# Attention feeding a channel mixer on one core: a fixed order of pieces in place of a planner, shared PSUM buffers, 1/rms by row tiles, q of two more batches by DMA transpose

## The chip, the cores and the metric

The kernel runs on one core of one Trainium2 chip. The metric is the time of one execution on the device in microseconds (us). Each kernel was run several times; a table gives the median and the range. The profile is one execution of its own; its span is about 2 us shorter than the reported time. An execution counts as slow when it is over 1.5% above the fastest of the same kernel; comparisons use the fast ones, and slow ones are pointed out.

Names used below: PE is the matrix engine, DVE the vector engine, ACT the scalar engine, POOL the engine that issues most loads, SP the engine that issues stores and DMA transposes. A "filler" is an idle matmul on zeros, whose only purpose is to keep PE's clock at full speed.

## The reference

Eight batches of eight heads; 576 positions; head size 64; so x has 8 × 576 rows of 512. All inputs and the output are float32.

```python
def attn(q, k, v, g_norm):                       # q, k, v: (8, 8, 576, 64)
    kv  = einsum('bhsd,bhse->bhde', k, v)        # 64 x 64 per head
    out = einsum('bhsd,bhde->bhse', q, kv)       # called u below
    rms = sqrt(mean(out * out, -1) + 1e-6)
    return out / rms * g_norm

def mixer(x, mu_k, mu_r, w_k, w_v, w_r):         # x: (8, 576, 512), from attn
    x_prev = x shifted by one position, zeros first
    xk = mu_k * x + (1 - mu_k) * x_prev
    xr = mu_r * x + (1 - mu_r) * x_prev
    k  = relu(xk @ w_k)                          # w_k: 512 x 1024
    v  = (k * k) @ w_v                           # w_v: 1024 x 512
    r  = sigmoid(xr @ w_r)                       # w_r: 512 x 512
    return r * v
```

## The kernel before

Matmuls run in bf16. Attention works by batch (0 to 7), the mixer by group of 512 rows (0 to 8), each as soon as its rows of xk and xr are there. In the text, "K of group 2" is the matmul of w_k with group 2's xk, "R" the one with w_r, "V" the one with w_v, and "u of batch 2" the matmuls of q with kv.

Every operation is a "piece" with its engine, its cost in us, what it depends on and the buffers it uses. A planner runs through the pieces with a list-scheduling model and decides the order, the engine of pieces that can go on either of two, and the buffers.

```python
class Planner:
    LAT = {"PE": 0.25, "ACT": 0.15, "DVE": 0.12, "POOL": 0.15, "SP": 0.0}
    ...
    def run(self, warm=None):
        ...  # picks the ready piece with the earliest start, then the earliest due time
             # puts fillers where PE would idle (before the first R, and until 80 us)

BUFS = { ...
    "mm": (2, (128, 2, 512), FP32),     # PSUM of the mixer
    "at": (2, (128, 2, 512), FP32),     # PSUM of attention
}
```

q has to be transposed before u. Batches 0 to 3 do that on PE, with a copy out of PSUM; batches 4 to 7 with a DMA transpose issued by SP:

```python
DMA_T = 4
...
if b >= DMA_T:
    def q_dma(_):
        nc.sync.dma_start_transpose(out=get(qT)..., in_=qin.t...)
else:
    for hp in hps:
        ...  nc.tensor.transpose(...)    # PE, into PSUM
        ...  copy(eng, get(qT)[...], ps.t[...])
```

1/rms is built from column sums of u squared (a matmul with a selector), Ln and Exp on ACT, and a matmul with a 0/1 selector that spreads it over all rows; DVE then multiplies three operands:

```python
nc.scalar.activation(out=get(ln), in_=pst.t[:, 0, 0:SEC], func=AF.Ln, bias=eps, scale=1.0 / HD)
nc.scalar.activation(out=get(rs), in_=ln.t, func=AF.Exp, scale=-0.5)
...
nc.tensor.matmul(get(ps)[:, i, SEC*c:SEC*c+SEC], selg[:, tl, sub]..., rs.t, start=True, stop=True)  # 144 columns each
nc.vector.scalar_tensor_tensor(out=xT..., in0=uT..., scalar=g_col, in1=ps..., op0=ALU.mult, op1=ALU.mult)
```

The run starts with loads by POOL, which also change float32 to bf16, and with fillers on PE:

```python
def idle(n, buf):
    for _ in range(n):
        nc.tensor.matmul(get(buf or warm)[:, 0, :], zeros[:, 0:128], zeros, start=True, stop=True)

plan.run((5.0, p_first, 80.0, idle))
```

## Time and profile before

| | before |
|---|---|
| time, median of 3 runs | 224.23 us (224.2 to 224.51) |
| span of the profile | 222.2 us |
| first R starts | 25.75 us |
| last matmul ends | 217.95 us |
| PE idle between the two | 6.7 us |
| fillers | 52 matmuls, 15.3 us |

From the page of the kernel before: the busy time of each engine, then rows of 40 equal slices of the span. Each digit is a busy share in tenths; PEclk is PE's granted clock in tenths of full speed; DMA is the mean busy share of the 16 DMA engines.

```profile
span 222.2 us, 4055 instructions
PE 205.6 (93%) x1671; PEld 102.5 (46%) x1671; DVE 144.8 (65%) x253; ACT 124.1 (56%) x172; POOL 25.8 (12%) x39
...
PE   2989999798799989999999999999999999999971
...
PEclk9999999999999999999999999999999999999999
DMA  5999999999999999999950420051033033033033
```

PE is busy nearly all the time, and at full clock from 10.7 us on. Before that the trace has no record of the clock, and the page draws a 9 there; six fillers took 2.74 us at 4.78 us, 0.46 us each, where later ones take 0.22. DMA is full for the first half of the run, then has slack. So PE is the limit, with the first 25 us and the DMA-full half as the places where something else can hold it up.

From the timeline of PE in the kernel before (start, duration, line, operands, shapes and count; in brackets the idle time before it and what ended that):

```profile
20.79 5.13 PE L620 MATMUL mm<-zeros 128*128 128x512 bf16 x23
25.75 1.89 PE L571 MATMUL mm<-w_r,xr 128*128 128x512 bf16 x8
28.01 0.95 PE L361 MATMUL at<-v,k 96*64 96x64 bf16 x48 [0.36 <-DMA v<-in_v_dram]
...
41.77 0.95 PE L361 MATMUL at<-v,k 96*64 96x64 bf16 x48 [1.22 <-DMA v<-in_v_dram]
...
72.83 1.89 PE L548 MATMUL mm<-xk,w_k 128*128 128x512 bf16 x8
```

The first R stands behind 23 fillers. Its data came in parts: the last xr that these eight matmuls read was written at 25.55 us (timeline of DVE). Batches 1 and 2 wait for their loads. K of group 2 starts at 72.83 us.

The chain of work that ended last (start, duration, what) has two DMA steps in the first 80 us, a load of q and a DMA transpose:

```profile
16.50 28.14 DMA q<-in_q_dram
...
63.59 12.60 DMA qT<-q
```

### The profile page before, as it was taken

To read this page: it belongs to the slowest core of one execution; us is meant where nothing else is said; L and a number is where in the kernel's file an instruction comes from. 1 tells how busy PE (TensorE), PEld (TensorE's weight loads), DVE (VectorE), ACT (ScalarE), POOL (GpSimd) and SP (SyncE) were. 2 spreads that over 40 slices of the span, in tenths; PEclk is the share of its full clock that TensorE was granted. 3 is DMA by queue.
4 is the path that set the end of the run, shared out by engine and by line. 5 is a ranking of instruction groups with operands and counts; after the bars stand their busy time and mean duration, and the time that the engine had idled before them with its cause. 6 is when DMAs were issued, how large, how long until landed. Compare 5 with 4: busy or idle time off the path is not lost.

```text
span 222.2 us, 4055 instructions
## 1 busy us (share of the span) xinstructions
PE 205.6 (93%) x1671; PEld 102.5 (46%) x1671; DVE 144.8 (65%) x253; ACT 124.1 (56%) x172; POOL 25.8 (12%) x39
## 2 busy tenths in 40 slices
PE   2989999798799989999999999999999999999971
PEld 1445454455354444545454694445444444444430
DVE  1159857358989999899679869976963143143131
ACT  5367647725948929776678277847716306405500
POOL 7861031210300500400000000000000000000000
PEclk9999999999999999999999999999999999999999
DMA  5999999999999999999950420051033033033033
GB/s 74 190 201 208 203 207 203 203 205 244 204 203 157 229 173 191 197 211 191 188 158 3 106 86 0 0 152 39 0 98 90 3 96 96 0 86 105 0 94 94
DMA packets 36150, 28.84 MB, mean 130 GB/s; under 512 B 11036, under 2 KB 31012, under 8 KB 36132
## 3 DMA queue, kind: packets, MB, share of 16 engines
q0 software_dynamic: 21008, 16.78, 49.3%
q1 hardware_dynamic: 15124, 11.81, 23.9%
q8 instruction: 13, 0.21, 0.4%
q14 instruction: 5, 0.04, 0.0%
HBM read 33.56 MB, written 9.44 MB: 193 GB/s over the span
## 4 chain that ended last, share of the span: by engine, by line
PE 71%; DMA 18%; DVE 6%; POOL 1%; issue 1%; ACT 0%; DVEq 0%; POOLq 0%
PE mm L591 27%; PE mm L548 22%; DMA q<-in_q_dram 13%; PE mm L571 11%; DMA qT<-q 6%; PE at L463 3%; PE mm L620 2%; PE at L411 2%; PE at L361 1%; DVE xT L471 1%; DVE out L595 1%; PE at L391 1%; PE at L440 1%; POOL k L294 1%; DVE sq L420 1%
## 5 line engine op out<-in xcount | busy, mean ns | idle before, releaser
L591 PE MATMUL mm<-w_v,sqk 128*128 128x512 bf16 x288 | 65.7, 379 | 1.7 <-DVE out L595 1.7
L548 PE MATMUL mm<-xk,w_k 128*128 128x512 bf16 (+1 forms) x320 | 66.1, 358 | 1.0 <-DVE xk L507 1.0
L552 ACT ACTIVATE relu<-mm 128x1024 bf16<-128x1024 f32 x36 | 36.7, 1024 | 44.5 <-PE mm L548 42.8
L548 PEld LDWEIGHTS <-w_k 128*128 128x128 bf16 x320 | 30.3, 98 | 29.6 <-issue 1.7
L591 PEld LDWEIGHTS <-sqk 128*128 128x128 bf16 x288 | 27.2, 98 | 34.1 <-issue 3.6
L555 DVE TENSOR_TENSOR sqk<-relu 128x1024 bf16<-128x1024 bf16 x36 | 24.7, 689 | 24.1 <-ACT relu L552 24.1
L595 DVE TENSOR_TENSOR out<-mm,sig 128x1024 f32<-128x1024 f32 (+1 forms) x20 | 22.1, 1116 | 24.9 <-PE mm L591 24.9
L571 PE MATMUL mm<-w_r,xr 128*128 128x512 bf16 x144 | 34.1, 379 | 0.0
L471 DVE SCALAR_TENSOR_TENSOR xT<-uT,mu_sb,at 128x576 bf16<-128x576 bf16 (+1 forms) x31 | 23.6, 791 | 3.0 <-PE at L463 2.7
L576 ACT ACTIVATE sig<-mm 128x1024 bf16<-128x1024 f32 x18 | 18.4, 1023 | 10.5 <-PE mm L571 10.4
L504 ACT ACTIVATE t<-d,mu_sb 128x576 bf16<-128x576 bf16 x30 | 21.0, 770 | 3.0 <-DVE xr L507 1.9
L571 PEld LDWEIGHTS <-xr 128*128 128x128 bf16 x144 | 13.3, 98 | 14.2
L221 ACT CAST uT<-at 128x576 bf16<-128x576 f32 x19 | 11.7, 637 | 9.4 <-PE at L411 9.4
L620 PE MATMUL mm<-zeros 128*128 128x512 bf16 x52 | 15.3, 423 | 0.0
L420 DVE TENSOR_TENSOR sq<-uT 128x576 bf16<-128x576 bf16 x32 | 13.3, 454 | 0.8 <-ACT uT L221 0.7
L294 POOL DMA_DIRECT2D k<-in_k_dram x10 | 7.5, 750 | 42.7 <-PE at L361 40.1
L463 PEld LDWEIGHTS <-selg 128*128 128x128 bf16 x128 | 9.6, 98 | 6.2 <-issue 1.2
L463 PE MATMUL at<-rs,selg 128*128 128x144 bf16 x120 | 11.1, 226 | 0.7 <-DVE xT L471 0.7
L507 DVE TENSOR_TENSOR xk<-t,xT 128x2304 bf16<-128x2304 bf16 (+2 forms) x10 | 11.2, 1118 | 0.4
L489 DVE TENSOR_TENSOR d<-xT 128x2304 bf16<-128x2304 bf16 (+2 forms) x10 | 11.2, 1119 | 0.3
L507 DVE TENSOR_TENSOR xr<-t,xT 128x2304 bf16<-128x2304 bf16 (+2 forms) x10 | 11.0, 1112 | 0.0
L502 DVE TENSOR_SCALAR t<-d,mu_sb 128x576 bf16<-128x576 bf16 x34 | 10.4, 368 | 0.2
(51 smaller groups left out, 133.1 us busy)
## 6 DMA issues: line engine op xcount, KB each, us to landing
out_dram<-out SPq DMA_DIRECT2D x24, 192.0 KB, 2.5
k<-in_k_dram POOLq DMA_DIRECT2D x7, 576.0 KB, 14.6
v<-in_v_dram POOLq DMA_DIRECT2D x7, 576.0 KB, 16.8
q<-in_q_dram POOLq DMA_DIRECT2D x7, 576.0 KB, 16.4
out_dram<-out SPq DMA_DIRECT2D x24, 128.0 KB, 2.4
out_dram<-out SPq DMA_DIRECT2D x24, 64.0 KB, 2.0
w_k<-in_moe_w_k_dram POOLq DMA_DIRECT2D x1, 1024.0 KB, 12.9
w_v<-in_moe_w_v_dram POOLq DMA_DIRECT2D x1, 1024.0 KB, 23.5
```

The lines of the kernel that those rows point to most:

```text
L463: nc.tensor.matmul(get(ps)[:, i, SEC * c:SEC * c + SEC], selg[:, tl, sub].rearrange("p e d -> p (e d)"), rs.t, start=True, stop=True)
L471: nc.vector.scalar_tensor_tensor(out=xT.t[:, hs, xs], in0=get(uT)[:, hs].rearrange("q h i jj p -> q h (i jj p)")[:, :, cs], scalar=g_col, ...
L504: nc.scalar.mul(out=dst, in_=d.t[:, hp, :], mul=by)
L507: nc.vector.tensor_tensor(out=dst[:, hsl, c0:c0 + S], in0=t.t[:, 0:n, :], in1=xT.t[:, hsl, 0:S], op=ALU.add)
L548: nc.tensor.matmul(get(ps)[:, fc % 2, a0:a1], w_k_sb[:, cc, 128 * fc:128 * fc + 128], xk[:, cc, x0:x0 + a1 - a0], start=(cc == 0), stop=(c ...
L552: nc.scalar.activation(out=get(rt), in_=ps.t, func=AF.Relu)
L555: nc.vector.tensor_mul(out=get(sqk)[:, 2 * f2:2 * f2 + 2, :], in0=rt.t, in1=rt.t)
L571: nc.tensor.matmul(get(ps)[:, ci % 2, :], xr[:, cc, n0:n0 + 128], w_r_sb[:, cc, :], start=(cc == 0), stop=(cc == NHP - 1))
L576: nc.scalar.activation(out=get(sg), in_=ps.t, func=AF.Sigmoid)
L591: nc.tensor.matmul(get(ps)[:, ci % 2, :], sqk.t[:, fc, 128 * ci:128 * ci + 128], w_v_sb[:, fc, :], start=(fc == 0), stop=(fc == NFC - 1))
L595: nc.vector.tensor_mul(out=get(ot)[:, xs, :], in0=ps.t[:, xs, :], in1=sg.t[:, xs, :])
L620: nc.tensor.matmul(get(buf or warm)[:, 0, :], zeros[:, 0:128], zeros, start=True, stop=True)
```

## The change

The intent, part by part:

1. The planner goes. A fixed list names every piece in order, with its engine and its buffer. The list was made ahead of time; the kernel only walks through it.
2. The two pairs of PSUM buffers become four that any piece may take.
3. Start: the first k and v come as float32 by the hardware queues of SP and ACT and are cast; 1/rms of batch 0 is done per head pair; R of group 0 accumulates head pair by head pair, so that it can begin before all of batch 0 is done.
4. 1/rms: one ACT function instead of Ln and Exp; sums and spreading as four row tiles (matmuls of 32 rows, 288 columns) instead of 144-column pieces; the factor g_norm moves into the selector, and DVE's three-operand multiply becomes a plain one.
5. q of batches 2 and 3 by DMA transpose too.
6. Few fillers: 25 at the start and 4 and 5 later, 224 columns each.

The diff, cut to its core:

```diff
-class Planner: ...
+ORDER = """
+    early_k::0 zero early_v::1 cast_v:A:0 cast_k:D:0 idle:25:0 kv0.0::0 load_k0.2 load_v0.2 ...
+    ... load_q0.2::0 load_q0.0 sel_load mu_load load_v0.4 ...
+    ... load_k2.0::0 load_v2.0::0 ... load_q2.0::0 ... qTd2::0 idle:5:0 V0.0a::0 ...
+    ... relu1.3::1 K1.5::3 u2.3::1 u2.2::2 ...
+"""                                  # 696 pieces: name:engine:buffers   (cut)
+class Plan:
+    def run(self, order, idle): ...  # walks through ORDER, checks dependencies and buffers
-    DMA_T = 4
+    DMA_T = 2
-        "mm": (2, (128, 2, 512), FP32),
-        "at": (2, (128, 2, 512), FP32),
+        "ps": (4, (128, 2, 512), FP32),
+    def load_early(n):               # first two heads of k and v: float32, then a cast
+        (nc.sync if eng == "SP" else nc.scalar).dma_start(out=raw..., in_=rows(n, 0, 0, 2))
-            nc.scalar.activation(out=get(ln), ..., func=AF.Ln, ...)
-            nc.scalar.activation(out=get(rs), in_=ln.t, func=AF.Exp, scale=-0.5)
+            nc.scalar.activation(out=get(rs)..., in_=get(pst)[:, :, 0:HS],
+                                 func=AF.Abs_reciprocal_sqrt, bias=1e-6, scale=1.0 / HD)
+            nc.tensor.matmul(get(pp[hp // 2])[:, hp % 2, 0:HS], sel[32*hp:32*hp+32]...,
+                             get(rs)[32*hp:32*hp+32, HS*half:HS*half+HS], start=True, stop=True)
-                    nc.vector.scalar_tensor_tensor(..., scalar=g_col, ..., op0=ALU.mult, op1=ALU.mult)
+                    nc.vector.tensor_tensor(..., op=ALU.mult)
+            for cc in range(NHP - 1):    # R of group 0, head pair by head pair
+                ms.append(add(f"R{g}.{cc}", ..., deps=ms[-1:] + [need["r"][cc], p_wr], bufs=pss))
-    plan.run((5.0, p_first, 80.0, idle))
+    plan.run(ORDER, idle)
```

## The prediction

> **What bounds the kernel now.** TensorE (PE 205.6 of 222.2 us in the busy-time table; DVE 65%, ACT 56%), in three stages.
> 1. Start: the first R matmul runs at 25.75 us (timeline); before it PE mostly runs 52 idle matmuls (15.3 us). From 15 to 25 us DVE is busy 9.65 us of 10 (windows): batch 0's norm chain is DVE-limited.
> 2. 25.75 to 217.97 us. The mixer's 720 matmuls at 0.864 us per four (chain of waits) are 155.5 us. The chain's increments give attention on PE: kv 0.88, u 0.8, sums 0.36, spreading 1/rms 1.1 per batch, PE transposes of q about 2.0 for batches 1 to 3; about 28 us. PE idles 5.0 us from 25.7 to 90 and twice 0.84 us in the tail, waiting for the output multiply.
> 3. End: 4.2 us from last matmul to end of span. The reported time is 2 us above the span.
>
> The DMA row is full to about 115 us at some 205 GB/s. kv of batch 2 waits for its load until 41.8 us; q of batch 2 lands at 44.6.
>
> **What the change does.**
> - Start: first loads by two hardware queues, 1/rms of batch 0 per head pair, R of group 0 per head pair. Batch 0 and w_r are 2.3 MB, 12 us at 205 GB/s after 3.5 us. DVE's list up to the last xr costs about 12 us by durations in the trace. Estimate: R starts at 16.5 us: -9.
> - PE: spreading takes four matmuls of 288 columns instead of eight of 144 per half; q of batches 2 and 3 goes to DMA transposes. I count 155.5 us mixer and 18.7 us attention from the first R on: -10.
> - DVE: x becomes a plain multiply (now 791 ns), squares go by two pairs (now 454 ns each). ACT: Ln plus Exp (0.70 us) become one. 13 table switches against 12 loads: nothing saved. Neither engine limits.
> - Shared PSUM buffers remove small waits only.
>
> **What is given back.** Loads carry the same bytes, so PE now runs into DMA. w_v lands at 34 to 36 us, when K of group 0 is done at about 30. q of batch 2 lands at 44.5; a DMA transpose took 12.6 to 15.2 us to land (DMA view), so u of batch 2 can't run before about 58, while the fixed order reaches it near 50. Batch 3's transpose queues behind (8 us of issue each). I expect 9 to 12 us of PE waits between 25 and 70 and K of group 2 starting near 69. Then 121 us mixer, 11.3 us attention, 1 us tail wait, 4.2 us end: span 205 (1 us taken off for overlap).
>
> **Predicted: 206.5 us, 8 in 10 from 199 to 212.** Faster by over 2%: 0.96; within 2%: 0.03; slower: 0.01.
>
> **What would show it.** Timeline: first R at 15 to 19 us, first K of group 2 at 65 to 71. Waits: several us of PE on DMA qT and w_v. After 70 us no PE gaps. PE filler about 5 us. DMA row full to about 110 us.
>
> **What would make it wrong.** If loads or transposes land earlier than the trace's rate says, the waits vanish: 197 to 199. If the fixed order, planned with modelled costs (relu 0.918 us where the trace has 1.02), stalls PE on PSUM or the in-order ACT and DVE queues: 210 or more. Few fillers may leave PE slow: the Trainium skill ("TensorE: Matmul & The Clock Gate", Part 1) says that after an idle window of about 3.4 us the clock halves; the first fillers here take 0.44 us against 0.22 later, which agrees. A cold R, or a cold stretch after the transpose wait, costs up to 1.7 us each.

The 1.7 us of its last sentence is an estimate: half of the page's window of 3.4 us.

## The result, and the profile after

| | before | after |
|---|---|---|
| time, median of 4 runs | 224.24 us (224.2 to 224.51) | 220.82 us (220.17 to 221.16) |
| ratio of fast runs, 95% interval | | 0.984 (0.982 to 0.986) |
| span of the profile | 222.2 us | 218.9 us |
| first R starts | 25.75 us | 20.85 us |
| K of group 2 starts | 72.83 us | 75.46 us |
| last matmul ends | 217.95 us | 213.38 us |
| mean granted PE clock | 1.000 | 0.946 |

Ratios here and below are the mean time of one kernel's fast runs over that of the kernel before in the same rounds, so they are not quite the ratio of the medians quoted. The change is 1.6% faster, which is within 2%; the prediction had 206.5 us and gave "within 2%" a chance of 0.03. It was wrong.

The same lines of the page, after:

```profile
span 218.9 us, 3677 instructions
PE 195.2 (89%) x1454; PEld 93.6 (43%) x1476; DVE 138.1 (63%) x251; ACT 125.2 (57%) x162; POOL 28.6 (13%) x45
...
PE   7277989999299999999988999999999999999970
...
PEclk9955799999859999999999999999999999999997
DMA  7999999999999990699999952220650004000485
```

PE has 10 us less to do, as busy time goes, but the span is only 3.3 us shorter. Two places catch the eye: PEclk falls to 5 in slices 3 and 4 (from about 11 to 22 us) and to 8 and 5 in slices 11 and 12 (55 to 66 us), and PE's row has a 2 in the first of these two (55 to 60 us).

The timeline of PE after:

```profile
11.33 0.56 PE L251 MATMUL ps<-ident,mu_raw 9*128 9x9 f32 x2 [2.73 <-DMA mu_raw<-in_moe_mu_r_dram]
...
21.70 3.69 PE L566 MATMUL ps<-w_r,xr 128*128 128x512 bf16 x10 [0.22 <-issue]
...
49.64 6.22 PE L544 MATMUL ps<-xk,w_k 128*128 128x512 bf16 x28
59.99 0.94 PE L392 MATMUL ps<-qT,kv 64*64 64x288 bf16 x12 [4.14 <-DMA qT<-q]
...
63.07 1.89 PE L600 MATMUL ps<-w_v,sqk 128*128 128x512 bf16 x4
...
69.67 1.04 PE L600 MATMUL ps<-w_v,sqk 128*128 128x512 bf16 x4
```

Three things are read here. A constants' transpose waits 2.73 us for a load. Ten matmuls of R take 3.69 us, where at full clock eight took 1.89 us before. And u of batch 2 (line 392) waits 4.14 us for the DMA transpose of q; the group of four matmuls 3 us later takes 1.89 us, and an equal one at 69.67, after the clock has come back, 1.04.

The chain of work that ended last, after:

```profile
42.24 1.96 PE ps L600 x9
44.20 15.75 DMA qT<-q
```

In the kernel before, the chain ran through the load of q to 44.6 us and then through PE; now it runs through the transpose until 59.95 us. The transposes' issue, from the timeline of SP after:

```profile
44.20 8.12 SPq L361 DMA_TRANSPOSE qT<-q  x1
54.54 2.06 SPq L526 DMA_DIRECT2D out_dram<-out  x4
56.83 14.38 SPq L361 DMA_TRANSPOSE qT<-q  x2
```

Stretches of both kernels: length, then busy time (and count) of PE, PE's weight loads, DVE, ACT and POOL, then granted clock, DMA share and GB/s. The kernel after:

```profile
10.00:25.00 15.00, 11.50 (x76) 5.89 (x78) 10.81 (x31) 9.85 (x19) 7.54 (x11) 0.54 1.27 202
...
40.00:60.00 20.00, 15.43 (x122) 6.79 (x121) 12.50 (x21) 9.79 (x13) 0.77 (x1) 0.96 1.31 190
60.00:80.00 20.00, 19.73 (x152) 8.11 (x155) 15.15 (x25) 10.90 (x15) 3.06 (x4) 0.86 1.17 195
```

The kernel before:

```profile
10.00:25.00 15.00, 13.65 (x128) 6.91 (x127) 11.37 (x28) 9.55 (x20) 5.50 (x7) 1.00 1.23 204
...
40.00:60.00 20.00, 16.21 (x229) 9.32 (x218) 14.01 (x25) 12.51 (x22) 3.83 (x5) 1.00 1.30 215
60.00:80.00 20.00, 19.15 (x198) 9.51 (x198) 18.53 (x34) 14.88 (x22) 3.80 (x4) 1.00 1.31 197
```

The 60 to 80 stretch shows why busy time misleads: PE is busier after than before (19.73 against 19.15 us), but at 0.86 of the clock. From 10 to 25 us PE is busy 77% of the time, and nearly all of it at half clock.

A balance of the span, all from the two timelines. "PE work" is busy time between the first R and the last matmul, with the cost of half clock taken out and given a row of its own. That cost is an estimate: half of the time at half clock after the first R (20.85 to 24.44 and 60.0 to 65.4 us), 4.5 us. The prediction's column is worked out from its own numbers.

| us | before | after | difference | predicted difference |
|---|---|---|---|---|
| first R starts | 25.75 | 20.85 | −4.9 | −9.2 |
| PE work from there | 185.5 | 177.6 | −7.9 | −11.3 |
| PE idle from there | 6.7 | 10.4 | +3.7 | +3.9 |
| half clock from there (estimate) | 0 | 4.5 | +4.5 | 0 |
| last matmul to the end | 4.25 | 5.5 | +1.3 | 0 |
| span | 222.2 | 218.9 | −3.3 | −16.7 |

One caution about the row "PE work". In the trace of the kernel after, 22 matmul records are missing (1454 matmuls for 1476 weight loads); the traces of before, k1 and k2 have all of theirs. k1 (below) has the same pieces and shows 179.5 us of work without its fillers (half of its 3.4 us of half clock taken out), where after shows 177.0 without its own. So the saving lies between 5.4 and 7.9 us, and the idle time and half clock of after are that much smaller.

This balance says where the time stands. It doesn't say what would help: whether an earlier R, for instance, would have shortened the span or only lengthened a later wait. That took experiments.

### The profile page after: what moved, and what is told of

Same layout as the page of the kernel before. It is cut to its first block, busy times and chain, and to the rows that moved or that the text cites. A ratio compares the mean times of both kernels' runs of the same rounds, so it can differ in the third digit from the quotient of the medians.

```text
span 218.9 us, 3677 instructions
## 1 busy us (share of the span) xinstructions
PE 195.2 (89%) x1454; PEld 93.6 (43%) x1476; DVE 138.1 (63%) x251; ACT 125.2 (57%) x162; POOL 28.6 (13%) x45
## 4 chain that ended last, share of the span: by engine, by line
PE 64%; DMA 17%; ACT 7%; DVE 5%; issue 2%; SPq 2%; DVEq 0%
PE ps L544 23%; PE ps L600 21%; DMA qT<-q 12%; PE ps L566 11%; PE ps L392 3%; DMA mu_raw<-in_moe_mu_r_dram 2%; DMA out<-in_k_dram 2%; PE ps L340 2%; SPq L526 2%; DMA out_dram<-out 1%; ACT kv L179 1%; ACT t L185 1%; PE ps L475 1%; DVE xT L480 1%; DVE out L604 1%
## 5 line engine op out<-in xcount | busy, mean ns | idle before, releaser
L600 PE MATMUL ps<-w_v,sqk 128*128 128x512 bf16 (+1 forms) x285 | 67.7, 377 | 2.0 <-DVE out L604 1.2
L544 PE MATMUL ps<-xk,w_k 128*128 128x512 bf16 (+1 forms) x314 | 66.4, 360 | 0.7 <-issue 0.4
L548 ACT ACTIVATE relu<-ps 128x1024 bf16<-128x1024 f32 x36 | 36.3, 1023 | 29.2 <-PE ps L544 28.2
L566 PE MATMUL ps<-w_r,xr 128*128 128x512 bf16 x139 | 36.5, 396 | 0.8 <-DVE xr L511 0.4
L604 DVE TENSOR_TENSOR out<-ps,sig 128x1024 f32<-128x1024 f32 (+2 forms) x21 | 22.2, 1066 | 13.5 <-PE ps L600 8.7
L571 ACT ACTIVATE sig<-ps 128x1024 bf16<-128x1024 f32 x18 | 18.2, 1022 | 12.0 <-PE ps L566 11.9
L480 DVE TENSOR_TENSOR xT<-uT,ps 128x576 bf16<-128x576 bf16 x28 | 19.9, 750 | 7.0 <-PE ps L475 6.9
L179 ACT CAST uT<-ps 128x576 bf16<-128x576 f32 x19 | 11.5, 640 | 12.0 <-PE ps L392 12.0
L501 DVE TENSOR_TENSOR d<-xT 128x1152 bf16<-128x1152 bf16 (+1 forms) x18 | 12.5, 692 | 0.6
L511 DVE TENSOR_TENSOR xk<-t,xT 128x1152 bf16<-128x1152 bf16 (+1 forms) x18 | 11.8, 685 | 0.3 <-ACT t L185 0.2
L511 DVE TENSOR_TENSOR xr<-t,xT 128x1152 bf16<-128x1152 bf16 (+1 forms) x18 | 11.8, 682 | 0.1
```

The lines of the kernel that those rows point to most:

```text
L480: nc.vector.tensor_tensor(out=get(xT)[:, 2 * i:2 * i + 2, NP + c:NP + c + HS], in0=flat(slice(2 * i, 2 * i + 2))[:, :, c:c + HS], in1=get( ...
L511: nc.vector.tensor_tensor(out=dst[:, hsl, c0:c0 + S], in0=get(t[key])[:, hsl, :], in1=get(xT)[:, hsl, 0:S], op=ALU.add)
L544: nc.tensor.matmul(get(ps)[:, fc % 2, a0:a1], w_k_sb[:, cc, 128 * fc:128 * fc + 128], xk[:, cc, x0:x0 + a1 - a0], start=(cc == 0), stop=(c ...
L548: nc.scalar.activation(out=get(rt), in_=get(ps), func=AF.Relu)
L566: nc.tensor.matmul(get(ps)[:, ci % 2, :], xr[:, cc, c:c + 128], w_r_sb[:, cc, :], start=(cc == 0), stop=(cc == NHP - 1))
L571: nc.scalar.activation(out=get(sg), in_=get(ps), func=AF.Sigmoid)
```

## The experiments

All kernels gave correct results. Those on the same chip share their runs of the kernel before. Milestones in us; "u2" is the first u of batch 2, "K2" the first K of group 2, "idle" is PE's between the first R and the last matmul, "half clock" the time at half clock from the first R on (b2's is read from the length of its matmuls, as its clock records begin only at 27.1 us; where a cell is empty the milestone was not read or has no plain counterpart).

| run | change | median (range) | ratio (95%) | R | u2 | K2 | idle | half clock |
|---|---|---|---|---|---|---|---|---|
| before | | 224.24 | | 25.75 | | 72.83 | 6.7 | 0 |
| after | | 220.82 (220.17–221.16) | 0.984 (0.982–0.986) | 20.85 | 59.99 | 75.46 | 10.4 | 10.4 |
| c1 | after, again | 220.32 (218.67–221.73) | 0.981 (0.976–0.987) | 20.13 | 59.72 | 75.47 | 11.0 | 8.1 |
| e1 | constants' load earlier | 218.72 (218.05–219.3) | 0.974 (0.971–0.977) | 17.81 | 59.72 | 75.27 | 11.5 | 13.4 |
| e2 | q of batch 2 on PE | 222.3 (220.62–223.66) | 0.990 (0.984–0.997) | 20.11 | 59.35 | 72.98 | 10.6 | 5.1 |
| e3 | fillers in the wait | 221.24 (218.41–223.74) | 0.976 (0.972–0.979) | 19.62 | 60.49 | 75.04 | 10.4 | 10.7 |
| e4 | late stores earlier | 218.76 (217.87–220.63) | 0.975 (0.971–0.980) | 19.85 | 60.53 | 76.32 | 11.9 | 12.6 |
| f1 | q of batch 2 loaded first | 221.44 (220.76–224.17) | 0.986 (0.981–0.991) | 20.20 | 55.99 | 76.23 | 11.4 | 10.7 |
| f2 | f1 and e1 | 220.43 (217.86–224.36) | 0.975 (0.967–0.982) | 18.07 | 56.86 | 74.44 | 12.6 | 6.2 |
| b1 | before, with q of batches 2 and 3 by DMA | 235.89 (234.96–237.3) | 1.053 (1.046–1.060) | 25.34 | | | 16.2 | 3.4 |
| b2 | before, without fillers | 224.44 (223.93–225.91) | 1.001 (0.996–1.006) | 22.88 | | 73.01 | 10.3 | 4.2 |
| e5 | q of batches 2 and 3 on PE | 223.23 (222.06–223.93) | 0.994 (0.990–0.998) | 19.75 | 60.14 | 76.03 | 12.1 | 4.0 |
| g1 | order planned anew, q of 2 and 3 on PE | 218.15 (217.63–219.8) | 0.973 (0.969–0.977) | 18.17 | 49.5 | 67.81 | 10.0 | 10.1 |
| g2 | order planned anew, q of 2 and 3 by DMA | 224.52 (221.54–226.95) | 0.992 (0.986–0.997) | 25.84 | | | 9.0 | 12.1 |
| g3 | as g1, model with shared DMA | 218.53 (215.44–218.75) | 0.970 (0.962–0.977) | 19.22 | 49.07 | 68.39 | 8.5 | 9.4 |
| g4 | as g3, no DMA transpose at all | 219.25 (218.47–220.32) | 0.978 (0.974–0.981) | 22.55 | | | 5.6 | 3.5 |
| h1 | e1 and e4 | 218.82 (218.07–220.21) | 0.976 (0.971–0.981) | 18.40 | 59.16 | 75.06 | 12.0 | 12.9 |
| k1 | h1 and fillers in both cold places | 217.41 (215.94–218.92) | 0.966 (0.964–0.969) | 17.74 | 60.36 | 74.93 | 5.8 | 3.4 |
| k2 | g3, batch 6 later, fillers at the start | 215.62 (214.48–216.35) | 0.960 (0.957–0.962) | 19.79 | 49.84 | 69.15 | 5.9 | 0 |

The medians of the kernel before are 224.24 to 224.58 us on all chips, so medians of different chips may be set side by side. Medians and ranges include slow executions, ratios don't. Slow executions: two of four in e3 (the profiled one among them), f2 and g2, one in f1 and g3. Kernels built on the kernel after scatter by up to 6.5 us from run to run, those built on the kernel before by about 2; a difference of 1 or 2 us between two of them is not much.

### Does an earlier start help? (e1)

The first theory: the constants' load stands behind eight small loads of the selector on one queue, which holds up batch 0 and makes R late. The rival: what is gained there is lost again in the wait for q of batch 2.

```diff
- load_q0.0 sel_load mu_load load_v0.4
+ load_q0.0 mu_load sel_load load_v0.4
```

> The changed kernel with one swap on the sync queue: the four small loads of mu and g are issued before the eight loads for the selector instead of after them. In the changed kernel the transpose matmul of mu waits 2.7 us for that load and R starts at 20.9 us. Theory A (the arrival of batch 2's DMA-transposed q at 60 us pins everything after it, so earlier gains are absorbed in the wait): R starts 2 to 4 us earlier, the wait of PE for that transpose grows from 4.1 us by about as much, and the time stays within 1 us of 220.8. Rival B (the late start is what the prediction missed): the time falls by 3 us or more, to 217.5 or less.

R started at 17.81 us, 3.0 earlier. The four kernels with this edit (e1, f2, h1, k1) begin R at 17.7 to 18.4 us, the seven others of this order at 19.6 to 20.9, so the load held R up by about 2 to 3 us. From the timeline of PE in e1:

```profile
59.72 0.94 PE L392 MATMUL ps<-qT,kv 64*64 64x288 bf16 x12 [7.14 <-DMA qT<-q]
```

The wait before u of batch 2 grew from 4.14 to 7.14 us, and u2 and K2 stayed where they were: what R gained was absorbed. (How far the wait grew is not sharp, as the repeat c1 has 5.76 us with R at 20.13; that u2 stays is.) The time, 218.72 us, lies between the two forecasts. The run as a whole is about 1 to 2 us better than after, with the difference late in the run (the 1.5 us wait for a later transpose at 115 us is gone); whether that comes from the edit or is scatter, I can't say.

### Is it the transposes of q? (e2, e5, b1, f1, f2)

If u of batch 2 waits for the DMA transpose, then transposing on PE, or loading q of batch 2 first, should take the wait away.

```diff
# e2: q of batch 2 on PE again, its pieces put in by hand; e5 does the same for batches 2 and 3
-    DMA_T = 2
+    DMA_T = 3
- ... qTd2::0 ...
- kvc2.0.0:A tk1.0:D xk1.2 R1.0::1 R1.1 xk1.0
+ kvc2.0.0:A qT2.0::3 qTc2.0:D:0 tk1.0:D xk1.2 R1.0::1 R1.1 qT2.1::3 qTc2.1:A xk1.0
- o0.1::3 K1.6::0 K1.7 relu1.0::0
+ o0.1::3 qT2.2::2 qTc2.2:D K1.6::0 K1.7 qT2.3::2 qTc2.3:A relu1.0::0
```

> The changed kernel with the transpose of batch 2's q put back on TensorE (four groups of transposes and four copies placed among the K and R pieces of group 1, as the kernel before has it); batches 3 to 7 stay on DMA. Costs PE about 1.2 us. Theory A: u of batch 2 runs at 50 to 54 us instead of 60, the 4.1 us wait and the half-clock stretch of 60 to 65.4 us (cost about 2.7 us) are gone, batch 3's transpose starts some 8 to 12 us earlier, and the time falls by 4 to 8 us, to 213 to 217. Rival B (late start and cold clock at the start): the time falls by no more than 1 us, or rises by 1.

> The changed kernel with q of batches 2 and 3 both transposed on TensorE again, by pieces inserted by hand into the otherwise unchanged order; about 2.4 us more PE work and 8 more copies on ACT and DVE. Theory A (the two early DMA transposes pin u of batches 2 and 3): no PE wait for a transposed q before 80 us, no half-clock stretch at 60 us; since the run with batch 2 alone on TensorE showed u of batch 2 still at 59 us behind the in-order copies, I expect a small gain only, 216 to 220. Rival B (late start): 221 to 224, slower by the added work.

e2 missed both of its forecasts. e5, at 223.23 us, fell into the range given for the rival (221 to 224). The wait for DMA was gone from this place, but u2 came at 59.35 and 60.14 us, as late as ever. From the timeline of PE in e2:

```profile
59.35 0.44 PE L393 MATMUL ps<-qT,kv 64*64 64x288 bf16 x8 [0.79 <-ACT relu L549]
```

Each engine runs its pieces in the order of the list, and the pieces put in by hand stood in a row with the others. Between 45 and 60 us PE of e2 now waited for ACT and DVE five times, 4.1 us in all: for copies of kv (1.22) and of q (0.73), a sigmoid (0.45), an output multiply (0.89) and a relu (0.79). In e2 K2 came 2.5 us earlier and the half-clock stretch there was gone, but 1.9 us of it went into a wait for a later transpose at 113.6 us. Here the pieces could not be moved alone with profit.

e2 also gives a measure of the half clock: it runs the same pieces from u2 to K2 at full clock, in 13.63 us, of which 0.48 is a wait for relu. The kernel after takes 15.47.

The other side of the same question: give the kernel before the transposes of the change. Its planner then makes a new order by itself.

```diff
# b1, on the kernel before
-    DMA_T = 4
+    DMA_T = 2
```

> The kernel before with one number changed: batches 2 and 3 too have q transposed by DMA instead of TensorE; its planner plans the rest anew. One part of the change alone. If DMA transposes this early cost more (15 us from issue to landing while loads fill the DMA engines) than TensorE gains (about 4 us of transposes), the time rises by 2 to 6 us above 224.2. If the part is worth what the change hoped, it falls by 2 to 4 us.

It took 235.89 us, 11.5 more than the kernel before and more than expected. The waits of PE (total us, times, longest) begin with:

```profile
PE at L411 <- DMA qT<-q: 5.1, 2, 2.9
```

PE idled 16.2 us where the kernel before idles 6.7, and ran 3.4 us at half clock after a wait. This is the only run that does one part of the change alone: on the kernel before, this part loses time. The planner's order isn't the fixed order, so 11.5 us isn't what it costs in the kernel after.

```diff
# f1: load q of batch 2 ahead of its k and v; f2: the same with e1's edit
- load_k2.0::0 load_v2.0::0 ... kvc1.2.1:D load_q2.0::0 ...
+ load_q2.0::0 load_k2.0::0 load_v2.0::0 ... kvc1.2.1:D ...
```

> The changed kernel with one load moved: q of batch 2 is loaded before k and v of batch 2 instead of after them, so it lands about 5.8 us earlier (two loads of 2.9 us) and its DMA transpose can start at about 38 instead of 44.2 us. Theory A (u of batch 2 is pinned by load plus transpose, everything after it by u): u moves from 60 to about 54 us, PE's wait there goes from 4.1 us to under 1, the half-clock stretch at 60 to 65 goes, K of group 2 starts at 69 to 71 instead of 75.5, and the time falls by 3 to 6 us, to 215 to 218. Rival B (late start and cold first R): nothing at the start changes, time within 1 us of 220.8.

> Both edits: mu loaded before the selector, and q of batch 2 before its k and v. Theory A: the 3 us that R gains at the start are again absorbed, now by a wait of 1 to 4 us before u of batch 2 at about 54 us; time within 1.5 us of the run that only loads q first. Rival B: 2 to 3 us below that run.

From the timeline of PE in f1:

```profile
55.99 0.56 PE L392 MATMUL ps<-qT,kv 64*64 64x288 bf16 x12 [0.68 <-DMA qT<-q]
...
73.92 0.70 PE L392 MATMUL ps<-qT,kv 64*64 64x288 bf16 x8 [6.11 <-DMA qT<-q]
```

And from that of SP in f1:

```profile
54.01 2.04 SPq L526 DMA_DIRECT2D out_dram<-out  x4
56.28 22.29 SPq L361 DMA_TRANSPOSE qT<-q  x2
```

The wait before u of batch 2 shrank from 4.14 to 0.68 us: the cause of that wait is shown. But batch 3's transpose still went out behind group 0's stores, at 56.28 us, and landed 17.6 us later, so u of batch 3 waited 6.11 us, and K2 came at 76.23, later than in after. The wait had moved from one batch to the next; 221.44 us is in the range of the rival, not of theory A. In f2 the two waits are 3.25 and 2.9 us, about the same sum. Yet its fast runs (two of four) average 218.75 us against 221.21 for those of f1, and that is the rival's forecast too. K2 comes 1.8 us earlier in f2, where half clock after the waits lasts 3.4 us instead of 6.8; with two fast runs, that this is the cause is not shown.

### What does the half clock cost? (e3, b2, k1)

The Trainium skill ("TensorE: Matmul & The Clock Gate", Part 1, "What's actually happening") says that PE runs at half clock by default and after an idle window of about 3.4 us, until it has been busy for such a window. The trace agrees in its form: matmuls of 512 columns take either about 0.22 us or about twice that, and the low stretches are about 6.8 and 13.7 us long. So the theory was: fillers where PE waits keep the clock and save half of each stretch.

```diff
# e3: 35 fillers in the wait
- K1.5::3 u2.3::1
+ K1.5::3 idle:35:1 u2.3::1
```

> The changed kernel with 35 idle matmuls of 224 columns (about 3.3 us at full clock) put just before u of batch 2, in the wait for the DMA transpose. If the half-clock stretch from 60 to 65.4 us comes from that wait and costs what I think, the granted clock stays at 1.00 there and the time falls by 2 to 3 us, to about 218. If the clock stretch is harmless (everything after it waits for something else), the clock is mended and the time stays within 0.7 us of 220.8.

The half-clock stretch shrank (61 to 64.4 us), and from u2 to K2 it took 14.55 instead of 15.5 us. The time is inconclusive: two of four runs were slow, the profiled one among them.

```diff
# b2, on the kernel before: no fillers at all
-    plan.run((5.0, p_first, 80.0, idle))
+    plan.run()
```

> The kernel before without its idle matmuls, nothing else changed in its plan. If they hold the clock and the start is on the path, the granted clock falls below 1.00 at the start, the first R matmuls and whatever runs until the clock returns take twice as long (some 2 to 4 us), and the time rises by 1.5 to 5 us. If it stays within 0.7 us of 224.2, idle matmuls were not needed in the kernel before.

R came earlier, at 22.88 us, and ran at half clock until 27.1, yet the time is the same as before's (ratio 1.001). The next kv waits for its load until 27.9 us in either case. In this start a cold PE costs nothing, since DMA sets the pace.

k1 puts fillers into both cold places of the kernel after, on top of e1's and e4's edits (h1, below):

```diff
+ idle:6:1 before mu_mm,  idle:12:3 before ss0.1,  idle:5:2 before ss0.0,
+ idle:4:3 before u0.2,   idle:4:1 before ss0.2,   idle:10:2 before u0.3
- K1.5::3 u2.3::1
+ K1.5::3 idle:70:1 u2.3::1
```

> The changed kernel with mu loaded first and the late stores moved (as in h1), and idle matmuls of 224 columns added: 41 in the gaps before R, 70 before u of batch 2 in the wait for its transposed q. The waits stay. If half clock costs what the ledger says (10 to 13 us of half-clock time after the first R, half of the busy part lost: 4 to 5 us), the clock stays at 1.00 through the R matmuls and u of batch 2 and the time falls to 213 to 216. If the clock is only a mark of the waits and everything after is bound elsewhere, 217.5 or more, as in h1 (218.8).

The mean clock rose to 0.988. From the timeline of PE in k1:

```profile
51.03 6.87 PE L646 MATMUL ps<-zeros 128*128 128x224 bf16 x70
60.36 0.56 PE L393 MATMUL ps<-qT,kv 64*64 64x288 bf16 x12 [2.46 <-DMA qT<-q]
```

Fillers filled most of the wait, and still the clock was at half from 61.8 to 65.2 us: the 2.46 us of idle that were left sufficed. The window of 3.41 us before the clock fell, in k1 (columns as in the stretches above):

```profile
58.39:61.80 3.41, 1.44 (x16) 0.57 (x15) 0.97 (x2) 0.95 (x2) 0.90 (x2) 1.00 1.16 254
```

How much idle time PE can afford comes out of the traces. Their clock records change only in steps of 3.41 us. I cut each of the 19 traces into these windows, from the first R on, and took PE's busy time in each. The clock fell after all 35 windows with 1.56 us busy or less, and after none of the 1016 with 1.63 us or more. It came back after all 22 with 3.08 us or more, and after none of the 25 with 2.66 or less. So a gap's place counts as well as its length: a gap of 2.54 us in e5 (115.0 to 117.5 us), shared between two windows with 2.50 and 1.78 us busy, cost no clock.

From u2 to K2 it took 14.57 us, against 15.9 in h1. Against h1 the median fell by 1.4 us (2.1 by the ratios), not the 4 to 5 expected; 217.41 us is between the two forecasts. Of the half clock's 4.5 us, then, 1.3 was got back at the second stretch; what the first had cost came to nothing, as R ran early only to wait for q of batch 2. u2 stands at 59 to 61 us in every kernel that keeps this order and these transposes, whether R begins at 17.7 or at 20.9 us.

### The end of the run (e4, h1)

```diff
# e4: two of group 5's stores ahead of group 6's
- ... o6.1::1 S6.2 S6.0 K7.4::3 ... S7.0 S7.1 S5.3 S5.2 V7.2b
+ ... o6.1::1 S5.3 S5.2 S6.2 S6.0 K7.4::3 ... S7.0 S7.1 V7.2b
```

> The changed kernel with the stores of half of group 5's output moved in the sync queue's order from behind the stores of group 7 to before those of group 6. In the changed kernel the output tile they hold comes free only at 210.7 us, so the next-to-last output multiply and the V matmuls behind it wait (PE 1.2 us), and 18 stores are issued after 203.9 us. If that order costs the tail: PE's gap at 210 to 211.5 goes, the end comes 2 to 3 us earlier, about 218. If the tail is bound by PE and by the issue of group 7 and 8's stores anyway: within 0.7 us of 220.8.

> The changed kernel with the two small edits tried singly before: mu loaded before the selector, and the late stores of group 5 moved forward. Singly they gave 218.7 and 218.8 against 220.8 and 220.3. If they are independent: 216 to 217.5. If both readings were within the spread or the gain at the start is absorbed as theory A says: 218 to 220.

In e4 the gap before the last V fell from 1.18 to 0.78 us, but it is 0.78 in e1 too, without this edit. The tail after the last matmul is 5.1 to 5.2 us in the three kernels with the edit (e4, h1, k1) and 5.5 to 6.3 in the eight others of this order, so the edit is worth some 0.4 us or more there; the medians of e4 and h1 are 2 us below after's, in the range of its scatter in c1. The two edits together do no better than either alone, as the second forecast for h1 had it.

### Another order (g1 to g4)

The remaining question was whether the pieces of the change could be faster in another order. I wrote a search over the order (swaps and moves, judged by a model of the engines with durations taken from these traces) and ran four results. Their lists differ from the kernel after's throughout, so they can't be shown as short diffs; the pieces are the same, apart from which batches transpose q on PE.

> The changed kernel itself once more, as a control for its spread, since variants of it scatter by up to 6 us between runs where the kernel before scatters by 1: both theories expect 219.5 to 222 us, with u of batch 2 at 59 to 61 us behind a wait for the transposed q.

> The changed kernel's pieces with q of batches 1 to 3 transposed on TensorE and the whole order searched anew against costs read from the traces. R starts at 16 to 19 us, u of batch 2 at about 49, K of group 2 at about 66, last V matmul at 203; 206 span, 208 us. If the theory is right that the order around the arrival of q of batches 2 and 3 ate the gain, 206 to 212 us; if a cause that my costs don't hold (engines contending, clock) ate it, 217 or more.

> The same search, but with DMA transposes from batch 2 on, as the change has it; the search then loads q of batch 2 before w_v, so that its transpose starts at 31 instead of 44 us and u of batch 2 runs at 48. Costs put it at 205 us, but the transposes have taken 15 to 18 us where loads fill the queues, and up to 22 us for two in a row, so I expect waits for batch 3's: 207 to 215 us. Worse than the order with TensorE transposes by 0 to 6 us if early DMA transposes are the harm; equal to or better than it if only the order was.

c1 came as expected. g1, at 218.15 us, fell into its second range (217 or more); g2, at 224.52, missed. g1 (q of batches 2 and 3 on PE) had K2 at 67.81 us, 7.7 earlier than after, and gave most of it back 25 us later. From the timeline of PE in g1:

```profile
95.50 1.49 PE L340 MATMUL ps<-v,k 96*64 96x64 bf16 x48 [5.28 <-DMA k<-in_k_dram]
```

And its stretches around that time:

```profile
80.00:90.00 10.00, 9.77 (x114) 4.49 (x112) 8.87 (x18) 7.61 (x11) 1.53 (x2) 1.00 1.10 145
90.00:100.00 10.00, 4.50 (x66) 2.50 (x60) 4.50 (x7) 3.58 (x7) 2.29 (x3) 0.66 1.38 155
```

k of batch 6 was issued at 81.11 us and landed after 95 us, while two DMA transposes were under way. DMA moved 145 and 155 GB/s in the two stretches, at shares of 1.10 and 1.38, where the kernel after moved 190 at 1.31 (40 to 60 us) and 202 at 1.27 (10 to 25 us). So the transposes didn't only land late; while these two ran, a load landed late as well. No run took the two transposes out of this stretch alone, but the DMA view, given a window, shows what they do to loads. Loads are q0, transposes and stores q1 (packets, MB, share of 16 engines). The kernel after, from 40 to 48 us, and then from 49 to 54 us:

```profile
q0 software_dynamic: 2157, 1.63, 131.4%
...
q0 software_dynamic: 767, 0.58, 87.1%
q1 hardware_dynamic: 849, 0.22, 47.6%
```

The loads fell from 203 to 116 GB/s (worked out: MB by time) when the transpose's packets came in, about one of theirs to one of the loads'. In g3 it is 142 GB/s for the loads from 92 to 98 us, with 1134 packets to 1133. And although the transpose was issued at 44.20 us, its first packet moved at 48.22. Half clock followed in g1 (93.1 to 99.9 us). g2 (q by DMA) is no clean counterpart: its order loaded q early and R began only at 25.84 us.

> The changed kernel's pieces, q of batches 1 to 3 transposed on TensorE, order searched anew with DMA transposes costed as sharing the DMA engines with the loads (about 4.7 us of their time each, from the wait seen in the previous replanned run), and long PE gaps penalised. K of group 2 near 67 us, no PE wait over 2 us for a load or a transposed q, end of the span near 208: 208 to 214 us. If the wait of 90 to 95 us only moves, 216 or more.

> The same search with every q transposed on TensorE: about 16 more transposes groups for PE (some 5 us) and 16 more copies, but no DMA transpose at all. Loads then land as fast as the queue gives them. PE should show no wait over 2 us for DMA after 40 us; K of group 2 near 68, end of the span near 212, 212 to 217 us. If PE has such waits without any DMA transpose, the transposes are not what gives the gain back.

g3, at 218.53 us, met the same wait for k of batch 6, 3.6 us long, and fell into its second range (216 or more). g4, at 219.25, missed its 212 to 217. With no DMA transpose at all, it had no wait of PE for DMA over 1.0 us after 40 us and 5.6 us of idle in all, but paid about 4 us more PE work (181.7 us against 177.6) and began R at 22.55 us.

### The best version (k2)

k2 is g3 with kv of batch 6 moved behind K of group 3 and 44 fillers spread before the first R (the PSUM buffers of some later pieces change with it, left out here):

```diff
- o2.0::0 ... xr3.0 kv6.0::2 kvc6.0.1:A:0 kvc6.0.2:A kvc6.0.0:A o2.1::3
+ o2.0::0 ... xr3.0 o2.1::3
- ... tr4.0::1 K3.4::2 u5.1::0 u5.2::1
+ ... tr4.0::1 K3.4::1 kv6.0::3 kvc6.0.1:A:0 kvc6.0.2:A kvc6.0.0:A u5.1::2 u5.2::0
+ idle pieces before kv0.3, mu_mm, ss0.0, ss0.3, u0.1, kv0.2, ss0.1, ss0.2
```

> The replanned order g3 with kv of batch 6, which waited 3.6 us for its load and let the clock fall for 6 us, placed after the next R and K pieces, and about 43 idle matmuls in the gaps before R. Costs from g3's trace: wait 3.6, half clock there about 3, half clock at the start about 1.3 us; so 218.5 minus 6 to 8: 210 to 213. If waits only move: 216 or more.

From the page of k2:

```profile
span 213.6 us, 3873 instructions
PE 197.6 (92%) x1559; PEld 97.7 (46%) x1559; DVE 137.0 (64%) x251; ACT 127.6 (60%) x168; POOL 28.8 (13%) x45
...
PE   7697799989999999979999999999999999999960
...
PEclk9969999999999999999999999999999999999995
```

From the timeline of PE in k2:

```profile
49.84 0.44 PE L393 MATMUL ps<-qT,kv 64*64 64x288 bf16 x8
...
69.15 1.03 PE L545 MATMUL ps<-xk,w_k 128*128 128x512 bf16 x4
```

u of batch 2 runs at 49.84 us, when PE reaches it, without a wait; K2 comes at 69.15 us; no half clock after R; idle 5.9 us. The median is 215.62 us, 4.0% below the kernel before, with an interval well clear of 2%, and below all other versions. Its PE work, 181.3 us, is 1.9 more than k1's without fillers, whose records are complete too; q of batches 2 and 3 is back on PE (52 transposes after the first R, 24 in k1). It still missed its expectation of 210 to 213 us, and since it has two edits over g3, what each is worth isn't shown.

## Why the prediction was wrong

The sum was: K of group 2 at 69, then 121 mixer, 11.3 attention, 1 tail wait, 4.2 end, less 1: a span of 205.5 us. The profile has 218.9. In order of the chain:

| step of the sum | predicted | measured | error |
|---|---|---|---|
| u of batch 2 | 58 | 59.99 | +2.0 |
| from there to K of group 2 | 11 | 15.5 | +4.5 |
| from there to the last matmul | 133.3 | 137.9 | +4.6 |
| last matmul to the end | 4.2 | 5.5 | +1.3 |
| "1 us taken off for overlap" | −1 | 0 | +1.0 |
| span | 205.5 | 218.9 | +13.4 |

- **The mechanism at the centre was right.** The transpose of q of batch 2 takes the DMA path at 44.2 us, lands 15.75 us later, and u waits for it. e1 shows that this wait takes up what the start gains; f1 shows that it is q's arrival that ends it. Its size was 2.0 us low.
- **"Batch 3's transpose queues behind"** was half right. It came late, at 56.83 us, but behind group 0's stores: the issue of batch 2's had ended at 52.32. In the kernel after nothing waited for it; f1 shows that it makes the waits hard to remove: with the first gone, the second is 6.11 us.
- **The step that failed most was "K of group 2 starting near 69".** It took the work after the wait at full clock, and I had my own sum wrong as well: e2 runs the same pieces from u2 to K2 at full clock in 13.1 us (13.63 less its wait), where 58 to 69 leaves 11. So 58 should have led to 71.1. Of the 4.5 us, then, 2.1 are work that the sum left out and 2.3 are half clock, measured as the difference between after and e2 (half of the 5.4 us would be 2.7). I had named the half clock as a risk, "up to 1.7 us each", and put none of it in the sum, although a wait of PE by several us was in the same sum. k1 shows the effect: with most of the wait filled, the same stretch is 1.3 us shorter.
- **"9 to 12 us of PE waits between 25 and 70"** was 5.9 us, 4.1 of them for q of batch 2; none was for w_v. With R 4.3 us later than said, the wait for q is shorter by about as much, so this is the other side of the late start and not a second error.
- **"After 70 us no PE gaps"** was wrong: 4.25 us of idle, 1.5 of them for a later DMA transpose (115.7 us), 1.2 in the tail. That is 3.2 us of the 4.6; the other 1.4 is PE work.
- **"PE: −10"** was mis-sized. From the first R on I counted 174.2 us of work; it was at least 177.6, and 180.1 by k1's complete records. The same way of counting gives 183.5 for the kernel before, where 185.5 was measured, so about 2 us of that is a count that is low for both, and the saving was 5.4 to 7.9.
- **"R starts at 16.5 us: −9"** was wrong by 4.3 us, 2 to 3 of them from the constants' load behind the selector's (e1). It cost nothing up to K of group 2, since the wait absorbed it. In the balance it looks like the second largest error; in the chain it is none. A term that is absorbed must not be counted as cause.
- **The end**: 4.2 taken over unchanged; the new end has more stores late (18 on SP in the last 15.1 us, 8 in the kernel before), and e4 got some 0.4 us of it back.
- Right as said: ACT and DVE don't limit, ACT's table loads save nothing (14, and 12 before), and PE waits for DMA before 70 us. The fillers came to 34 matmuls of 224 columns, 5.5 us, with 5 predicted.

What stays open: the later part of e1's gain; how much of after's run-to-run spread comes from where its gaps fall in the clock's windows; and why k2 is still 3 us over its own model. That a DMA transpose slows the loads beside it is measured; that this alone made k of batch 6 late in g1 and g3 is argued, as no run isolates it.

## What to carry to other kernels

Moving work from a busy engine to a DMA path helps only if its result is wanted later than that path delivers while loads are under way; read the landing time from the trace under the same load, and check the next transfer in the queue as well. When a sum has a wait of several us of the matrix engine in it, put the half clock after it into the sum, and don't credit a gain ahead of a fixed arrival: up to there it only lengthens the wait. In a fixed order, undo a part by planning the order anew, not by moving its pieces by hand: e2 and e5 took the wait away and gained nothing, g1 gained 7.7 us at the same place.

## What the Trainium skill lacked or had wrong

- "Advanced Engine Details and Errata", section "X-Bar Transpose (TRN2)", says that transpose DMAs are as fast as regular ones and expects 350 to 400 GB/s. The transpose of one batch's q is 0.59 MB (8 × 576 × 64 × 2 bytes) and took 15.75 us from issue to landing beside loads, about 37 GB/s worked out, and 10.47 us (about 56 GB/s) for one that the chain shows from 105.20 us on; 12.60 us in the kernel before. These times hold waiting and sharing, so they don't refute the page. The fairest case is g1 from 82 to 84 us, where transposes had the queues almost alone: 0.36 MB, 181 GB/s, against 203 GB/s for the loads alone (after, 40 to 48 us). That is nearly the loads' rate, as the page says, but half of its figure. What a transpose does to loads beside it is on no page that I read: the loads fell from 203 to 116 GB/s in the kernel after and ran at 142 in g3, with packets of both about one to one.
- How long the issue of a DMA transpose holds its queue is missing there too ("DMA: Bandwidth & Descriptors" counts sequencer cycles, for "previous generations"): 8.12 us for one beside loads (after, 44.20 us), 22.29 us for two in f1, and 3.63 to 4.09 us for the last three of the kernel after.
- "TensorE: Matmul & The Clock Gate", Part 1, says that for modelling the cost of the ramp is under 1% of a typical span. The ramp at R fits (an estimate: 1.8 of 218.9 us, half of 3.6); the second stretch added 2.3 us, so both together are about 2%, though k1 got only 1.4 us back. Part 1 speaks of idle and busy windows and doesn't say how much activity makes one. Here, from the first R on, 1.56 us busy of 3.41 was too little and 1.63 enough to keep the clock, and 3.08 brought it back. In k1 a gap of 2.46 us, shorter than the page's window, sufficed. Before the first R, with small matmuls, these limits don't hold: windows with up to 2.38 us busy lost the clock (g2), and from 10 to 25 us in the kernel after PE was busy 11.50 of 15 us at a mean clock of 0.54 (Part 4 says that transposes don't count as busy in the same way, which may be part of it; no run here tells the two apart).
- "ScalarE: Activation LUTs", "What ACT_TABLE_LOAD costs", gives 1283 ns for the load, which the trace confirms, and about 1380 ns of drain on top, which it doesn't show. From the timeline of ACT in the kernel after, where the load starts as the casts end (100.41) and the sigmoid follows at once:

```profile
98.50 1.91 ACT L179 CAST kv<-ps 64x256 bf16<-64x256 f32 x5
100.43 1.28 ACT L571 ACT_TABLE_LOAD   x1
101.72 1.02 ACT L571 ACTIVATE sig<-ps 128x1024 bf16<-128x1024 f32 x1
```
